# One level of Strassen for the second FFN product of two batches, and a new order of pieces, in an attention and FFN kernel

## The chip, the cores and the metric

The kernel runs on one core of a Trainium2 chip. The core has a matrix engine (PE; the loading of its stationary operand is listed as PEld), a vector engine (DVE), a scalar engine (ACT), a general engine (POOL) and a queue engine for transfers (SP). Each works through its own list of instructions in order and waits on semaphores for the others. SBUF is the on-chip memory, PSUM the eight banks into which PE writes. The metric is the device time of one execution in microseconds; of the kernel before there are three runs, with a median of 164.83 us (164.77 to 165.41).

## The reference

Eight batches of eight heads, 576 tokens, head dimension 64, 32 memory slots. With a softmax over the tokens, phi compresses keys and values to 32 rows; the queries attend to these; the outcome, 4608 tokens by 512, goes through a feed-forward network whose hidden layer is the maximum of three products.

```
a = exp(phi - max(phi, axis=2)); a = a / (sum(a, axis=2) + 1e-09)
k_m = einsum('bhsm,bhsd->bhmd', a, k);  v_m = einsum('bhsm,bhsd->bhmd', a, v)
scores = q @ k_m.T / sqrt(64);  attn = softmax(scores) @ v_m
x = attn.transpose(0, 2, 1, 3).reshape(4608, 512)
h = maximum(maximum(x @ w1, x @ w2), x @ w3)      # 512 -> 768
out = h @ w_out                                   # 768 -> 512, float32
```

## The kernel before

A batch is 576 tokens. Its compressed values are folded into the weights, so that the FFN works on the attention weights themselves: `fold` makes wp (for w1 - w3 and w2 - w3) and wp3 (for w3 times w_out), `ffn1` makes the hidden layer as max(a, max(b, 0)) of the differences, and `ffn2` adds the w3 part back: out = h @ w_out + attn @ wp3. In `ffn2` one tile of 128 tokens is eight matmuls of 512 columns in one PSUM bank: six over the hidden layer and two over attn. Each loads its own 128 by 128 stationary block. Two batches make 1152 tokens, nine tiles: T0 to T3 of each, and T4, which lies across both. A finished bank is copied to a tile `ot` in SBUF and stored by SP, 256 KB a tile.

The program is a written-out list of pieces, each a letter, a number and a batch: `F8@2` is step 8 of ffn1 for batch 2. Every engine executes its share of the pieces in the order of the list; nothing reorders them later. The pieces that matter here:

- L0, L1, L2, L3 load phi, K, V and q of a batch (L88 to L112). POOL issues them, so they stand in POOL's order with POOL's arithmetic. All loads go through one queue. H2, H0, Y and so on are the first batch's parts and the weights.
- E is the exponential of phi (ACT). r1 and r0 are POOL copies of V and K of batch 2 and later into an interleaved tile `kvr` (L102). B (PE) compresses K and V (for batches 0 and 1, in two parts straight from the loaded tile: B0 for K with the sums, B1 for V), N normalizes (DVE), K transposes on PE and copies.
- Q0 and Q1 transpose q (DVE), S are the scores (PE) and two exponentials (ACT); a, s, c are a transpose, a sum and a reciprocal (DVE) for each of two groups, m multiplies (POOL, L406), X transposes back into `attn` (DVE, L416).
- D0 to D3 are the folds, F0 to F11 ffn1 (an even one ends in a copy by ACT, an odd one in a maximum by DVE, both out of PSUM), T0 to T4 ffn2. O prepares w3 times w_out from the transposed w3 in `w3T`. U, A and P do not exist yet. A mark `!` swaps ACT for DVE or back in a piece that copies.
- A PSUM bank for each piece comes from a written-out string of digits.

A load may be issued only when what it overwrites has been read: K and V have two tiles, for even and odd batches, and phi and q two each. The loads of batch 2 overwrite what batch 0 used.

```
for w in """ ... """.split():
    n, b = w.rstrip("!").split("@")
    issue(int(b), n, w.endswith("!"))
```

## Time and profile before

| | us |
|---|---|
| median of three runs | 164.83 |
| span of the profiled execution | 163.3 |
| PE busy | 153.8 |
| ACT busy | 100.6 |
| DVE busy | 90.4 |
| POOL busy | 69.5 |
| ffn2's matmuls, 512 columns, L497 and L506 | 51.3 and 18.4 |
| ffn1's matmuls, L466 | 50.5 |
| V of batch 7 has landed | 111.8 |
| last matmul ends | 159.6 |

The page of the profiled execution gives its span, from the first to the last instruction, and no other time of it; the median of the runs lies 1.53 us above. All times inside the trace count from the span's start. A row of the timeline gives start, duration, engine, line, operation, output and inputs, and in brackets how long the engine stood idle before it and what ended that. A row of the stretches gives, behind the stretch's length, the busy time and the number of instructions of PE, PEld, DVE, ACT and POOL, then the granted clock of PE, the share of the DMA engines (above 1 where transfers overlap in one engine) and GB/s. A row of the chain gives start, duration and the work. Where a time of a named piece is given, it was found by counting PE's matmuls along the list. Landing times are the completion events of the transfers in the trace.

### The profile page before, as it was taken

The page shows a single profiled execution, that of the slowest core. Times are in us where ns is not written, and L with a number is a line of the kernel's source. Part 1 is how long each engine was busy: PE and PEld are TensorE (multiplying, and loading weights), DVE is VectorE, ACT ScalarE, POOL GpSimd, SP SyncE. Part 2 cuts the span into 40 slices and gives each one's busy share as a digit, 9 for nine tenths or more (in the row PEclk, how much of TensorE's full clock was granted, in tenths as well). Part 3 has the DMA queues.
Part 4 walks back from the last instruction along what each step waited for, and adds up shares of the span by engine and source line. Part 5 has one row for each costly group of instructions (what it writes and reads, how often), then busy time and mean ns, then how long its engine had stood idle before and what let it go on. Part 6 is the DMA issues. An engine that isn't in the chain of part 4 may idle for free.

```text
span 163.3 us, 4838 instructions
## 1 busy us (share of the span) xinstructions
PE 153.8 (94%) x2080; PEld 85.3 (52%) x2080; DVE 90.4 (55%) x181; ACT 100.6 (62%) x151; POOL 69.5 (43%) x71
## 2 busy tenths in 40 slices
PE   7978798899899999999999999999999999999990
PEld 2433444564377436743673575576553468744450
DVE  2023704798838665849399748879749128810010
ACT  4205445845497488778885899994658976223320
POOL 7932205100599259657968957646403100000000
PEclk9999999999999999999999999999999999999998
DMA  6999999999999999999999999996313130014333
GB/s 150 152 206 207 205 210 217 274 208 210 253 313 238 209 253 379 274 210 293 252 263 206 232 355 264 191 233 150 130 69 129 69 128 0 0 68 186 135 128 130
DMA packets 21974, 31.77 MB, mean 195 GB/s; under 512 B 1216, under 2 KB 16576, under 8 KB 21952
## 3 DMA queue, kind: packets, MB, share of 16 engines
q0 software_dynamic: 16080, 21.43, 68.7%
q1 hardware_dynamic: 5728, 9.90, 17.2%
q8 instruction: 16, 0.26, 0.6%
q10 hardware_dynamic: 144, 0.13, 0.2%
q14 instruction: 6, 0.05, 0.1%
HBM read 39.32 MB, written 9.44 MB: 299 GB/s over the span
## 4 chain that ended last, share of the span: by engine, by line
PE 83%; DMA 9%; POOL 2%; ACT 2%; issue 1%; DVE 1%; ACTq 0%; POOLq 0%
PE psum L497 29%; PE psum L466 28%; DMA wo_sb<-in_moe_w_out_dram 9%; PE psum L506 8%; PE psum L440 6%; PE psum L249 4%; PE psum L192 3%; PE psum L333 2%; PE psum L515 1%; ACT h L170 1%; PE psum L538 1%; PE psum L298 1%; POOL kvo L97 1%; ACT wp L172 1%; POOL qq L110 0%
## 5 line engine op out<-in xcount | busy, mean ns | idle before, releaser
L497 PE MATMUL psum<-wo_sb,hT 128*128 128x512 bf16 x210 | 51.3, 380 | 0.0
L466 PE MATMUL psum<-attn,wp 128*128 128x288 bf16 x384 | 50.5, 286 | 0.1
L479 DVE TENSOR_TENSOR hT<-psum,h 128x576 bf16<-128x576 f32 x48 | 34.2, 749 | 18.0 <-PE psum L466 12.5
L466 PEld LDWEIGHTS <-wp 128*128 128x128 bf16 x384 | 36.7, 98 | 13.2 <-issue 2.0
L172 ACT COPY ot<-psum 128x512 f32<-128x512 f32 x35 | 20.7, 591 | 32.1 <-PE psum L506 25.2
L497 PEld LDWEIGHTS <-hT 128*128 128x128 bf16 x210 | 19.2, 97 | 24.0 <-issue 4.3
L172 ACT CAST wp<-psum 128x1024 bf16<-128x1024 f32 (+1 forms) x31 | 29.2, 995 | 3.8 <-PE psum L440 2.0
L103 POOL COPY kvr<-kvo 128x2304 bf16<-128x2304 bf16 x12 | 25.3, 2111 | 13.7 <-DMA kvo<-in_k_dram 10.1
L170 ACT ACTIVATE h<-psum 128x576 bf16<-128x576 f32 x47 | 28.4, 659 | 3.5 <-PE psum L466 3.3
L409 POOL TENSOR_TENSOR t<-t,sm 128x576 bf16<-128x576 bf16 x14 | 16.1, 1154 | 24.6 <-DVE sm L404 24.4
L506 PE MATMUL psum<-wp,attn 128*128 128x512 bf16 x62 | 18.4, 379 | 0.0
L159 PE MATMUL psum<-warm 128*128 128x512 bf16 x44 | 12.1, 427 | 1.2 <-DVE warm L128 1.2
L313 DVE STREAM_TRANSPOSE qT<-qq 128x576 f32<-128x576 f32 x16 | 11.7, 747 | 1.4 <-DMA qq<-in_q_dram 1.4
L342 ACT ACTIVATE e<-psum 128x576 bf16<-128x576 f32 x16 | 9.6, 652 | 3.8 <-PE psum L333 3.8
L229 ACT ACTIVATE e<-ph 128x1152 bf16<-128x1152 f32 (+1 forms) x9 | 9.6, 1065 | 1.7 <-DMA ph<-in_phi_dram 1.6
L395 DVE TENSOR_REDUCE sm<-t 128x18 f32<-128x576 bf16 x14 | 10.3, 738 | 0.2
L387 DVE STREAM_TRANSPOSE t<-e 128x288 f32<-128x288 f32 x14 | 6.4, 465 | 6.2 <-ACT e L342 6.1
L97 POOL DMA_DIRECT2D kvo<-in_v_dram x9 | 6.7, 749 | 7.1 <-PE psum L249 4.1
L506 PEld LDWEIGHTS <-attn 128*128 128x128 bf16 x62 | 6.1, 98 | 7.1
L110 POOL DMA_DIRECT2D qq<-in_q_dram x8 | 6.2, 770 | 6.6 <-DVE h L174 3.7
L555 DVE COPY ot<-psum 128x256 f32<-128x256 f32 x1 | 0.4, 425 | 15.4 <-PE psum L546 15.4
L249 PEld LDWEIGHTS <-e 64*32 64x32 bf16 x720 | 6.9, 90 | 3.7 <-issue 3.3
(57 smaller groups left out, 114.4 us busy)
## 6 DMA issues: line engine op xcount, KB each, us to landing
out_dram<-ot SPq DMA_DIRECT2D x35, 256.0 KB, 5.6
qq<-in_q_dram POOLq DMA_DIRECT2D x8, 576.0 KB, 12.2
ph<-in_phi_dram POOLq DMA_DIRECT2D x7, 576.0 KB, 14.4
kvo<-in_k_dram POOLq DMA_DIRECT2D x7, 576.0 KB, 14.6
kvo<-in_v_dram POOLq DMA_DIRECT2D x7, 576.0 KB, 15.6
w_sb<-in_moe_w_dram POOLq DMA_DIRECT2D x3, 768.0 KB, 19.0
wo_sb<-in_moe_w_out_dram POOLq DMA_DIRECT2D x1, 768.0 KB, 14.6
ph<-in_phi_dram SPq DMA_DIRECT2D x2, 288.0 KB, 3.0
```

The costliest lines, as they stand in the source:

```text
L103: nc.gpsimd.tensor_copy(out=kvrs[b % 2][:, :, :, D * i : D * (i + 1)], in_=kvos[b % 2][:, 1 - i])
L159: nc.tensor.matmul(po[:, 0:BANK], lhsT=warm[:, 0:P], rhs=warm, start=True, stop=True)
L170: nc.scalar.activation(out=out_, in_=in_, func=AF.Relu)
L172: nc.scalar.copy(out=out_, in_=in_)
L249: nc.tensor.matmul(kvp[M * j : M * (j + 1), a, 0:nd], lhsT=s["e"][r, j, c, :], rhs={None: lambda: kvr[r, j, c, 0:nd], 0: lambda: k_and_one ...
L313: nc.vector.transpose(out=s["qT"][:, j].rearrange("p j c r e -> p (j c r e)").bitcast(FP32), in_=loaded[b]["q"][:, j].rearrange("p j c d - ...
L395: nc.vector.tensor_reduce(out=sm, in_=s["t", g].rearrange("p n r e -> p n e r"), op=ALU.add, axis=mybir.AxisListType.X,)
L409: nc.gpsimd.tensor_tensor(out=t, in0=t, in1=s["sm", g].unsqueeze(2).to_broadcast([P, S // HP, R, 2]), op=ALU.mult,)
L466: nc.tensor.matmul(acc[:, h, 0:SH], lhsT=wps[b][:, g, w * DF + ft * P : w * DF + (ft + 1) * P], rhs=attn[:, g, c0 : c0 + SH], start=(g == ...
L479: nc.vector.tensor_tensor(out=hT[:, ft, (b % 2) * S : (b % 2 + 1) * S].rearrange("p (h n) -> p h n", h=2), in0=a, in1=s["h1", ft], op=ALU.max,
L497: nc.tensor.matmul(po, lhsT=hT[:, fc, c0 : c0 + P], rhs=wo_sb[:, fc, :], start=(n == 0), stop=False,)
L506: nc.tensor.matmul(po, lhsT=attn[:, g, c0 : c0 + P], rhs=wp3s[b][:, g, :], start=False, stop=(g == NG - 1),)
```

## The change

For batches 5 and 6, T0 to T3 are replaced by seven products P0 to P6. The left matrix is the batch's four token tiles, 512 tokens by 1024 (768 of h and 256 of attn), the right one is w_out over wp3, 1024 by 512. Both are cut in two by two blocks: tokens into tiles 0 and 2 against 1 and 3, the inner dimension into 512 and 512 (three hidden tiles and one of attn each), the columns into 256 and 256. One level of Strassen's method in its form with fifteen additions needs seven block products for these in place of eight. A product is eight matmuls of 256 columns (four inner tiles by two token tiles).

What is new beside the products: U makes four differences of the blocks of w_out once (U0 to U3 at "batch 9", 768 elements in each partition, in the place of `w3T`, which is free after O0@0) and four of wp3 for each of the two batches (256 elements). A makes four sums or differences of h (A0 to A3, 768 elements) and four of attn (A4 to A7, 256 elements) for each batch. They are bf16; each runs on DVE or POOL as the list says: U on DVE where marked, A on POOL where marked. Three of the products' results are copied to SBUF while their bank goes on accumulating, three output blocks are made by a DVE addition of PSUM and such a copy, one by a plain copy. The store is two transfers of 512 KB a batch instead of four of 256 KB.

The tile of ones beside K and V moves ahead of K, and K and V change places in their tile; `opool` has four tiles in place of six. The order of pieces is a new one from N0@1 on, and the string of banks with it. The list's first pieces, up to N0@1, are unchanged. Shown are the new code, and of the two lists the old one's beginning of batch 1 and the new one from the same place on.

```diff
-    opool = ctx.enter_context(tc.tile_pool(name="opool", bufs=6))
+    opool = ctx.enter_context(tc.tile_pool(name="opool", bufs=4))
...
-    kvos = []
-    for i in range(2):
-        kvo = const.tile([P, 3, NP, NC, D], BF16, name=f"kvo{i}")
-        kvos.append(kvo)
+    KV = NP * NC * D
+    ones_k = [const.tile([P, D + 2 * KV], BF16, name=f"kvo{i}") for i in range(2)]
+    kvos = [
+        x[:, D:].rearrange("p (i j c d) -> p i j c d", i=2, j=NP, c=NC) for x in ones_k
+    ]
...
-            out=kv[:, 1 - i, h].rearrange("p j c d -> p j (c d)"),
+            out=kv[:, i, h].rearrange("p j c d -> p j (c d)"),
...
-            out=kvrs[b % 2][:, :, :, D * i : D * (i + 1)], in_=kvos[b % 2][:, 1 - i]
+            out=kvrs[b % 2][:, :, :, D * i : D * (i + 1)], in_=kvos[b % 2][:, i]
...
-    for kvo in kvos:
-        nc.vector.memset(kvo[:, 2, 0, 0], 1.0)
+    for x in ones_k:
+        nc.vector.memset(x[:, 0:D], 1.0)
...
-    def k_and_ones(kv, r, j, c):
-
-        flat = kv[r].rearrange("p i j c d -> p (i j c d)")
-        k0 = (NP * NC + j * NC + c) * D
-        step = 2 * NP * NC * D - k0
-        return flat[:, k0 : k0 + 2 * step].rearrange("p (i x) -> p i x", i=2)[:, :, 0:D]
+    def ones_and_k(b, r, j, c):
+        step = D + (j * NC + c) * D
+        return ones_k[b % 2][r, 0 : 2 * step].rearrange("p (i x) -> p i x", i=2)[:, :, 0:D]
...
+    KT = FT // 2
+    CH = DM // 2
+    TW = 2 * P
+    SUB, ADD = ALU.subtract, ALU.add
+    B11, B12, B21, B22 = [
+        (slice(KT * i, KT * (i + 1)), slice(CH * j, CH * (j + 1)))
+        for i in range(2)
+        for j in range(2)
+    ]
+    tw = w3T.rearrange("p f j n -> p (f j n)").rearrange("p (i k c) -> p i k c", i=4, k=KT)
+    sa0 = const.tile([P, 4, TW], BF16, name="sa0")
+    oj0 = [const.tile([P, 2, DM], FP32, name=f"oj{i}") for i in range(2)]
+    SNAP = {0: "m5", 1: "m1", 4: "u2"}
+    twb, sas, quads = {}, {}, {}
+    def combine(on_dve, out_, in0, in1, op):
+        eng = nc.vector if on_dve else nc.gpsimd
+        eng.tensor_tensor(out=out_, in0=in0, in1=in1, op=op)
+    def combine_w(b, i, on_dve):
+        if b == B + 1:
+            x = {n: wo_sb[:, n[0], n[1]] for n in (B11, B12, B21, B22)}
+            t = [tw[:, n] for n in range(4)]
+        else:
+            if b not in twb:
+                twb[b] = work.tile([P, 4, CH], BF16, name="twb")
+            w = wp3s[b]
+            x = {n: w[:, n[0].start // KT, n[1]] for n in (B11, B12, B21, B22)}
+            t = [twb[b][:, n] for n in range(4)]
+        in0, in1 = [(x[B12], x[B11]), (x[B22], t[0]), (x[B22], x[B12]), (x[B21], t[1])][i]
+        combine(on_dve, t[i], in0, in1, SUB)
+    def sums(b):
+        if b not in sas:
+            if b == B - 1:
+                s = inp.tile([P, NP, NC, D], BF16, name="sx", tag="qq")
+                s = s.rearrange("p j c d -> p (j c d)").rearrange("p (i n) -> p i n", i=3)
+                sa = inp.tile([P, NP, NC, D], BF16, name="sy", tag="qq")
+                sa = sa.rearrange("p j c d -> p (j c d)")[:, 0 : 4 * TW]
+                sa = sa.rearrange("p (i n) -> p i n", i=4)
+            else:
+                s, sa = w_sb[:, 0:3, 2], sa0
+            sas[b] = (
+                s.rearrange("p i (k q n) -> p i k q n", k=KT, q=2),
+                sa.rearrange("p i (q n) -> p i q n", q=2),
+            )
+        return sas[b]
+    def blocks(x, b, k):
+        c0 = (b % 2) * (S + HP)
+        x = x[:, :, c0 : c0 + 2 * TW]
+        return [
+            [
+                x[:, k * i : k * (i + 1)].rearrange("p f (q r n) -> p f q r n", q=2, r=2)[
+                    :, :, :, r
+                ]
+                for i in range(2)
+            ]
+            for r in range(2)
+        ]
+    def combine_a(b, i, on_dve):
+        s, sa = sums(b)
+        n = i % 4
+        if i < 4:
+            (a11, a12), (a21, a22) = blocks(hts[b // 2], b, KT)
+            t = {0: s[:, 0], 1: s[:, 1], 2: a21, 3: s[:, 2]}
+        else:
+            (a11, a12), (a21, a22) = blocks(attns[b // 2], b, 1)
+            t = {m: sa[:, m : m + 1] for m in range(4)}
+        in0, in1 = [(a21, a22), (t[0], a11), (a11, a21), (a12, t[1])][n]
+        combine(on_dve, t[n], in0, in1, ADD if n == 0 else SUB)
+    def products(b, i, swap):
+        s, sa = sums(b)
+        h, a = blocks(hts[b // 2], b, KT), blocks(attns[b // 2], b, 1)
+        wp3 = wp3s[b]
+        def plain(r, c):
+            return lambda k, q: h[r][c][:, k, q] if k < KT else a[r][c][:, 0, q]
+        def summed(n):
+            src = h[1][0] if n == 2 else s[:, min(n, 2)]
+            return lambda k, q: src[:, k, q] if k < KT else sa[:, n, q]
+        def w_plain(i, j):
+            c = slice(CH * j, CH * (j + 1))
+            return lambda k: wo_sb[:, KT * i + k, c] if k < KT else wp3[:, i, c]
+        def w_summed(n):
+            return lambda k: tw[:, n, k] if k < KT else twb[b][:, n]
+        lhs, rhs, name = [
+            (summed(0), w_summed(0), "y"),
+            (plain(0, 0), w_plain(0, 0), "x"),
+            (plain(0, 1), w_plain(1, 0), "z"),
+            (summed(3), w_plain(1, 1), "y"),
+            (summed(1), w_summed(1), "x"),
+            (summed(2), w_summed(2), "x"),
+            (plain(1, 1), w_summed(3), "x"),
+        ][i]
+        acc = quads.setdefault(b, {})
+        if i < 3:
+            acc[name] = one_bank()
+        po = acc[name]
+        for k in range(KT + 1):
+            for q in range(2):
+                nc.tensor.matmul(
+                    po[:, q * CH : (q + 1) * CH],
+                    lhsT=lhs(k, q),
+                    rhs=rhs(k),
+                    start=(i < 3 and k == 0 and q == 0),
+                    stop=(k == KT and q == 1),
+                    skip_group_check=True,
+                )
+        x = po.rearrange("p (q n) -> p q n", q=2)
+        def copy(out_, in_):
+            if swap:
+                nc.vector.tensor_copy(out=out_, in_=in_)
+            else:
+                nc.scalar.copy(out=out_, in_=in_)
+        if i in SNAP:
+            t = ln if i == 0 else work.tile([P, S], FP32, name="snap", tag="r")
+            t = acc[SNAP[i]] = t[:, 0:DM].rearrange("p (q n) -> p q n", q=2)
+            copy(t, x)
+        if i == 2:
+            if b == B - 1:
+                ot = [inp.tile([P, NP, NC, M], FP32, name=f"ox{n}", tag="ph") for n in range(2)]
+                acc["ot"] = [
+                    x.rearrange("p j c m -> p (j c m)")[:, 0 : 2 * DM].rearrange(
+                        "p (q n) -> p q n", q=2
+                    )
+                    for x in ot
+                ]
+            else:
+                acc["ot"] = oj0
+        if i not in (2, 4, 5, 6):
+            return
+        ot = acc["ot"][i // 5][:, :, slice(0, CH) if i in (2, 6) else slice(CH, DM)]
+        if i == 6:
+            copy(ot, x)
+        else:
+            if i == 4:
+                x = acc["y"].rearrange("p (q n) -> p q n", q=2)
+            y = acc[{2: "m1", 4: "u2", 5: "m5"}[i]]
+            nc.vector.tensor_tensor(out=ot, in0=x, in1=y, op=ADD)
+        if i in (4, 6):
+            r0 = b * S + (b % 2) * HP
+            rows = out[r0 : r0 + 2 * TW].rearrange("(q r p) c -> p q r c", q=2, r=2)
+            nc.sync.dma_start(out=rows[:, :, i // 5], in_=acc["ot"][i // 5])
 
...
+            "U": lambda: combine_w(b, i, swap),
+            "A": lambda: combine_a(b, i, not swap),
+            "P": lambda: products(b, i, swap),
...
-        L0@1 V1@0 F1@0 E@1 F3@0 L1@1 F5@0 F9@0 F7@0 L3@1 F11@0 B0@1 T3@0 N0@1 K0@1! L2@1 Q1@1
-        L2@2 L1@2 Q0@1 L0@2 V2@0 T0@0! L3@2 S@1 T1@0 a0@1 s0@1 c0@1 m0@1 B1@1 N1@1 a1@1 L1@3
-        K1@1 s1@1 D0@1 D1@1! D2@1 c1@1 m1@1 X0@1 L3@3 r1@2 X1@1 T2@0! L2@3 F6@1 F10@1 F7@1 F2@1
-        F3@1 F4@1 F0@1 r0@2 E@2 F5@1 F1@1 F11@1 L0@3 L0@4 F8@1 L2@4 F9@1 B@2 D3@1 N@2 Q1@2
-        T0@1! K@2 T2@1! r0@3 Q0@2 S@2 a0@2 a1@2 s1@2 c1@2 m1@2 T4@1! D1@2! s0@2 D2@2 c0@2 m0@2
-        X1@2 D0@2 T3@1 Q0@3 L3@4 X0@2 Q1@3 T1@1 F0@2 F4@2 F8@2 F6@2 F9@2 E@3 F7@2 r1@3 F5@2
...
+        D2@0 D4@0 F4@0 L0@1 V1@0 F1@0 E@1 F3@0 L1@1 F5@0 F9@0 F7@0 L3@1 F11@0 B0@1 T3@0
+        N0@1 U0@9 Q0@1 Q1@1 K0@1 V2@0 T0@0 S@1 L2@1 B1@1 a0@1 T1@0 s0@1 L0@2 N1@1 c0@1
+        a1@1 K1@1 s1@1 c1@1 m1@1! D0@1 L2@2 L1@2 m0@1 L3@2 D1@1! X0@1 X1@1 D2@1! T2@0!
+        F6@1 F4@1! F10@1 F0@1! F7@1 E@2 r1@2 F8@1 L1@3 F11@1 F5@1 F1@1 F9@1 F2@1 r0@2
+        F3@1 B@2 D3@1 T0@1! N@2 K@2! Q1@2 L2@3 Q0@2 T2@1 L0@3 S@2 a0@2 a1@2 s0@2 T4@1!
+        L0@4 D1@2! s1@2 D2@2! E@3 c0@2 D0@2 T1@1 L3@3 T3@1 L2@4 r0@3 r1@3 D3@2 B@3 c1@2
+        m1@2! X1@2 m0@2 X0@2 F8@2 F2@2 N@3 Q0@3 F3@2 F4@2 F6@2 Q1@3 F5@2 F0@2 F9@2 F1@2
+        F10@2 F7@2 F11@2 K@3 E@4 T2@2 L3@4 Q1@4 S@3 a0@3 T1@2 L1@4 L2@5 a1@3 s1@3 c1@3
+        L3@5 L0@5 D1@3! r1@4 D0@3 L1@5 L0@6 Q0@4 r0@4 D2@3 s0@3 m1@3 c0@3 L1@6 T0@2!
+        m0@3! D3@3 B@4 X1@3 L2@6 T3@2 X0@3 F8@3 U2@9 N@4 F4@3 L3@6 K@4! Q0@5 F5@3 F9@3
+        F10@3 r1@5 F0@3 F11@3 S@4 F1@3 F2@3 a1@4 r0@5 a0@4 F6@3 U1@9 F3@3 E@5 F7@3 s0@4
+        D0@4 D1@4! c0@4 T3@3 B@5 s1@4 c1@4 m0@4 D3@4 D2@4 m1@4 r0@6 X0@4 T0@3! X1@4 F4@4
+        N@5 F10@4 Q1@5 L0@7 L1@7 F5@4 F0@4! r1@6 F8@4 F11@4 F2@4 K@5 U3@9 F6@4 E@6 F9@4
+        L2@7 S@5 T4@3! Q1@6 Q0@6 D2@5 a1@5 a0@5 s0@5 D3@5 B@6 L3@7 T2@3! N@6 s1@5 F3@4
+        r0@7 c0@5 c1@5 F7@4 m1@5 F1@4 K@6! E@7 T1@3! S@6 a0@6 U0@5! m0@5 D1@5! T0@4!
+        X1@5 s0@6 D0@5! X0@5 D1@6! D3@6 r1@7 T3@4 F4@5 a1@6 B@7 Q0@7 D2@6 s1@6 D0@6 U0@6
+        N@7 A4@5! T1@4 c1@6 m1@6 F5@5 F8@5 F2@5 F6@5! F9@5 U1@5 A5@5 K@7! F0@5 F7@5 F1@5
+        F3@5 F10@5 F11@5 T2@4! Q1@7 A7@5! A0@5 X1@6 D0@7! U2@6! S@7 c0@6 a1@7 s1@7 T4@5!
+        U2@5 D2@7 D3@7 A6@5! A1@5! A2@5 a0@7 m0@6 A3@5! D1@7! U3@5 P0@5! P1@5! X0@6
+        P2@5! P3@5 F2@6 s0@7 c1@7 c0@7 m1@7! m0@7 A4@6! P4@5 F4@6 X1@7 F6@6 P5@5 A5@6!
+        X0@7 F10@6 A6@6 F3@6 F8@6 P6@5 F9@6 F5@6 F0@6 F11@6 F10@7 F7@6 F1@6 F2@7 A7@6!
+        F8@7! A0@6! F4@7 F11@7 U1@6 F9@7 F3@7 F5@7 P0@6! F0@7! F6@7! A1@6! A3@6 F1@7
+        P1@6 P2@6! A2@6 F7@7 P3@6! P4@6 T0@7! T4@7! T1@7! P5@6! T2@7! U3@6 P6@6! T3@7
```

## The prediction

> **What bounds the kernel now.** I read the page's busy shares first, then busy times by stretch, then GpSimd (POOL) in order of time, then the chain.
>
> ```profile
> span 163.3 us, 4838 instructions
> PE 153.8 (94%) x2080; PEld 85.3 (52%) x2080; DVE 90.4 (55%) x181; ACT 100.6 (62%) x151; POOL 69.5 (43%) x71
> DMA  6999999999999999999999999996313130014333
> ```
>
> PE is busy 94%, but the DMA row is full too, up to slice 27 (about 112 us). So there are two near-bounds. The stretches:
>
> ```profile
> 38.00:42.00 4.00, 4.00 (x86) 1.64 (x83) 3.45 (x5) 2.41 (x6) 0.00 (x0) 1.00 1.21 210
> 46.00:159.60 113.60, 113.56 (x1451) 65.03 (x1449) 68.04 (x135) 78.76 (x117) 52.44 (x43) 1.00 0.78 191
> 116.40:159.60 43.20, 43.18 (x405) 23.69 (x383) 16.31 (x29) 23.58 (x37) 2.27 (x2) 1.00 0.26 95
> 159.60:163.30 3.70, 0.00 (x0) 0.00 (x0) 0.00 (x0) 0.37 (x1) 0.00 (x0) 0.78 0.32 109
> ```
>
> From 46 us to the end PE idles 0.04 us of 113.6: whatever it must wait for lengthens the kernel, whatever it need not compute shortens it. The DMA share of 1.21 at 38 to 42 us is a full load queue. POOL feeds that queue and also multiplies:
>
> ```profile
> 24.74 0.74 POOL L97 DMA_DIRECT2D kvo<-in_v_dram  x1 [4.08 <-PE psum L249]
> 25.47 0.75 POOL L97 DMA_DIRECT2D kvo<-in_k_dram  x1
> 26.79 0.75 POOL L93 DMA_DIRECT2D ph<-in_phi_dram  x1 [0.57 <-issue]
> 31.21 0.74 POOL L110 DMA_DIRECT2D qq<-in_q_dram  x1 [3.66 <-DVE h L174]
> 42.42 1.16 POOL L409 TENSOR_TENSOR t<-t,sm 128x576 bf16<-128x576 bf16 x1 [10.47 <-DVE sm L404]
> 43.53 0.80 POOL L97 DMA_DIRECT2D kvo<-in_k_dram  x1
> 44.45 1.15 POOL L409 TENSOR_TENSOR t<-t,sm 128x576 bf16<-128x576 bf16 x1
> 46.35 2.12 POOL L103 COPY kvr<-kvo 128x2304 bf16<-128x2304 bf16 x1
> 49.14 2.12 POOL L103 COPY kvr<-kvo 128x2304 bf16<-128x2304 bf16 x1
> ```
>
> All four loads of batch 2 (V, K, phi, q) are issued by 32 us; then POOL stands 10.47 us in front of m0@1. Under that wait the queue works: by the trace's completion events q1 lands at 37.69, V1 40.53, V2 44.11, K2 48.47, phi2 50.03, q2 53.47, and so on without a gap to V7 at 111.80 and q7 at 114.64. The packs r1@2 and r0@2 (46.35, 49.14) end at 51.26; B@2 starts at 51.94, when the twelve F@1 are done. Matmul prices, from the chain:
>
> ```profile
> 146.82 0.43 PE psum L506 x2
> 152.43 1.29 PE psum L497 x6
> 157.73 0.76 PE psum L538 x6
> 158.49 0.22 PE psum L546 x2
> ```
>
> A 512-column matmul takes 0.215 us, a 256-column one 0.11 (the 0.76 has a 0.1 us start in it), although each loads its own weights.
>
> **The change, part by part.** *Products.* Per batch 4 tiles x 8 x 0.215 = 6.91 us go and 7 x 8 x 0.11 = 6.14 us come: minus 0.77, for two batches minus 1.53 us, all on PE. L538 has the same size and weight pattern, so I take 0.11. The new order also changes less often between 128-row and tiled pieces (0.1 us each): minus 0.2.
>
> *Combinations.* A 768-element difference costs 0.56 us on DVE (from 1024 elements in 0.684 and 2048 in 1.198), 1.54 on POOL (from 576 in 1.154); 256 elements 0.3 and 0.5. From about 110 us on POOL gains 12 us of these (12 x 0.5, 4 x 1.54), DVE 3.4, 4 us of PSUM additions (6 x 0.67, from 0.749 for 576) and 2.5 of copies. The third stretch above has 41 us of POOL and 27 of DVE free; cost 0. If a product waited for its last difference, it would be A1 then A3 (POOL, 3 us after A0, 1.15 more for m0@6): up to 1.5 us per batch. That is the upper bound; the lower is 0. PSUM reuse between products has 0.9 to 2.6 us of other matmuls against a copy of 0.59. The four differences of w_out (U@9, 1.54 each on POOL) lie among the loads: U0@9 and U1@9 are followed below, U2@9 and U3@9 stand in front of L3@6 and L2@7, which the full queue hides; without it 1.5 us each.
>
> *Small parts.* The ones beside K instead of behind V: B@0 and B@1 keep 72 matmuls of 128 columns, 0. Four output tiles in place of six: a T comes each 1.73 us at most, four in 6.9, a store lands in 5.6 (median) or 7.6 (the longest): 0, at worst 0.7 for a copy. T0@0, T2@1 and T2@2 are copied by DVE (0.67) and not by ACT (0.59): no PSUM bank of theirs is wanted within 0.9 us, 0.
>
> *Order before B@2: what decides.* The new POOL order is L3@1, U0@9, L2@1, L0@2, **m1@1**, L2@2, L1@2, **m0@1**, L3@2, r1@2, L1@3, r0@2. U0@9 waits for O0@0 (26.3 on PE) and takes 1.54, so L2@1 is issued at 28 instead of 19.92; as K1 and q1 still hold the queue until 37.69, V1 lands at 40.5 as before, phi2 at 42.1. But V2 and K2 now stand behind m1@1. That needs q1 (37.69), two transposes, S@1, the exponentials and, in DVE's new order, a0, s0, N, c0, a1, the K1 copy, s1, c1. T1@0 now runs between B1@1 and K1@1 on PE, so the K1 copy is at 43.4, c1 ends at 44.65. m1@1 runs 44.75 to 45.9, L2@2 is issued at 45.9, L1@2 at 46.65, m0@1 ends at 48.55.
> Two consequences. X0@1 needs m0@1: F6@1 starts at 49.1, not 45.96; PE stands still for 2.9 us. And the load queue is empty from 42.1. From issue to first packet the first load took 2.44 us (1.25 to 3.69), and a full load behind another runs 2.84 (37.69 to 40.53 for V1): V2 lands at 51.2, r1@2 ends at 53.4; L1@3 0.75; K2 landed at 54.0; r0@2 ends at 56.3. The F@1 end at 55.1. **B@2 starts at 56.4, plus 4.5 us.** Bounds: F6@1 alone gives 55.1 (plus 3.2); 1 us more in the queue gives 57.4.
> The Trainium skill ("DMA: Bandwidth & Descriptors", section on the anatomy of one DMA) gives about 2.0 us plus bytes over 436 GB/s for a GpSimd-issued DMA. As an estimate that puts V2's 1.18 MB at 50.6 and the sum 0.6 us lower; the trace's first load, above, speaks for the longer figure.
>
> *Order after B@2.* Old work left on PE is 159.58 - 51.94 = 107.64 us; new 107.64 - 1.53 - 0.2 = 105.9. So PE ends at 162.3 without further waits. Further waits by the same bookkeeping: E@3 on ACT now stands before D0@2's copy and waits for phi3 (66), so T3@1's copy and F8@2 slip 0.5; q3 is issued behind phi3 and phi4 and lands near 71.5, and DVE's Q0@3 is in front of F3@2's maximum: 0.4; m0@3 stands behind r0@4 (K4, 81), m1@3 and L1@6: F8@3 slips 0.7; m0@4 and m1@4 behind U1@9: F4@4 slips 0.4. Sum 2.0. A second way: the load queue of the old trace has no gap to make up time in, so the 3.5 us by which q2 is late (57.0 against 53.47) reach V7: it lands at 115.3, r1@7 ends at 117.4 and B@7 starts then. The new list has 46.8 us of PE pieces from B@7 on (35 F 17.2, 14 products 12.3, 8 T 14.5, the rest 2.8): 164.2, that is 1.9 us of further waits. I take 1.9, as the stream is the harder limit. Bounds 0 (the stretch above shows no PE wait of this kind) and 4.
>
> *The end* stays: T3@7 in two halves, 3.7 us from PE's last matmul to the span's end. P6@6's 512 KB go out on SP 1.4 us before; the old T4@7 put 256 KB there. 0 to 0.5; I take 0, since the last half leaves from ACT's queue.
>
> Sum: plus 4.5 - 1.7 + 1.9 = plus 4.7 us; the span goes from 163.3 to 168.0. The median of the runs is 164.83, 1.53 above the span of the profiled execution; with that distance kept, **169.5**.
>
> **Rivals.**
> *The saving arrives (faster).* If V2 and K2 are packed by the old 51.26, only minus 1.7 us remain: 163.1. It needs POOL free of m1@1 before about 40 us. For it: the queue runs ahead everywhere else. Against it: m0@1 in the old order, with less in front of it, could not start before 42.42. Chance 0.07. A halved wait (plus 2.2 at B@2, nothing after) gives 165.3, no change: 0.04.
> *The load stream falls further back.* Between B@2 and B@7 the old trace has 64.5 us, the new pieces at their prices 58.9 (37 F of 0.49, 14 T of 1.73, 2 T4 of 1.94, the small pieces and changes 12.7): the new order wants V7 sooner after B@2 than the old. With 3.5 us of lag V7 is just what B@7 waits for; each further us that POOL's packs lose it, standing before later loads until their own data land, is a us at the end. With 3 us more: 172.5. Chance 0.1.
> *Products wait for differences late.* 1.5 us per batch on top of the forecast: 172.5. For: DVE holds F maxima beside them. Against: the free time above. Chance 0.07.
> *PE's clock falls in the 2.9 us gap.* In the last stretch the mean granted clock is 0.78 of 3.70 us, which is 2.1 us at 1.00 and then 0.50: it fell 2.1 us after the last matmul. In the gap at F6@1 3.4 us at half clock would stretch the F@1 to 56.8; B@2 then slips only 0.4, since it waits for r0@2 anyway: 169.9. It is counted inside the forecast, at evens.
> The Trainium skill ("TensorE: Matmul & The Clock Gate", Part 1) has the clock halve after an idle window of about 3.4 us; by that rule a 2.9 us gap would leave it whole and the time at 169.5. The 2.1 us of the trace speak against waiting that long.
>
> **How the numbers follow.** The forecast with its bounds has 0.72: 169.5, own range 166.3 (B@2 at plus 3.2, no later wait) to 172.6 (plus 5.5, later waits 4). The stream (0.1) and the late products (0.07) end at 172.5; 0.04 is no change, 0.07 faster. The range 166.2 to 172.6 leaves out the last two and the upper halves of the two before, 2 in 10. Within 0.5% (0.8 us) is about what a measurement here cannot tell from no change. Faster 0.07, same 0.04, slower 0.89.
>
> **What will show it.** POOL's L2@2 after the first multiplication of batch 1 and near 46 us; a gap of PE of about 3 us before the first F@1 and of 1 us before B@2, ended by a copy on POOL; B@2 near 56.4; product matmuls of 256 columns 0.11 us apart; PE's end near 164. Wrong if L2@2 is issued before 42 us, if B@2 starts before 54, or if the products run at more than 0.12 us a matmul.

## The result, and the profile after

The changed kernel takes 174.64 us (median of four runs, 174.00 to 175.26), the kernel before beside it 164.91 (164.77 to 165.41): 1.056 times as long, interval 1.049 to 1.063. The forecast was 169.5 with 166.2 to 172.6 about it: the sign is right, the size is not, and the time lies above the range. The profiled execution is the longest of the four, 0.6 us above their median. Of the runs below, one with two issues moved (172.07 us) and one with both batches' products (172.64 us) were over 1.5% slower than the fastest of their kernel; the medians take in all runs, the ratios leave these two out.

The page of the changed kernel, its span, busy times, granted clock and DMA row:

```profile
span 173.3 us, 4949 instructions
PE 156.0 (90%) x2128; PEld 91.2 (53%) x2128; DVE 109.2 (63%) x211; ACT 92.0 (53%) x135; POOL 90.5 (52%) x91
PEclk9999999999978999999999999999999999999999
DMA  5999999996199999999999999999310303200635
```

The DMA row, solid before up to slice 27, now has a hole, above all at slice 10 counted from 0 (43 to 48 us): the load queue ran empty. Just behind it the clock dips. POOL in order of time shows why the queue was empty:

```profile
26.70 1.64 POOL L503 TENSOR_TENSOR w3T<-wo_sb 128x768 bf16<-128x768 bf16 x1 [8.77 <-PE psum L193]
28.30 0.78 POOL L98 DMA_DIRECT2D kvo<-in_v_dram  x1
...
45.05 1.15 POOL L409 TENSOR_TENSOR t<-t,sm 128x576 bf16<-128x576 bf16 x1 [15.22 <-DVE sm L404]
46.16 0.79 POOL L98 DMA_DIRECT2D kvo<-in_v_dram  x1
46.94 0.75 POOL L98 DMA_DIRECT2D kvo<-in_k_dram  x1
...
52.85 2.10 POOL L104 COPY kvr<-kvo 128x2304 bf16<-128x2304 bf16 x1 [3.25 <-DMA kvo<-in_v_dram]
...
56.26 2.11 POOL L104 COPY kvr<-kvo 128x2304 bf16<-128x2304 bf16 x1 [0.62 <-DMA kvo<-in_k_dram]
```

POOL stands 15.22 us in front of m1@1, and only then issues V and K of batch 2. V2 lands at 52.80, K2 at 56.20. What PE waits for, the rows of its timeline with idle time in front:

```profile
49.52 7.87 PE L466 MATMUL psum<-attn,wp 128*128 128x288 bf16 x48 [2.79 <-DVE attn L417]
58.42 0.80 PE L248 MATMUL psum<-kvr,e 64*32 64x129 bf16 x72 [1.02 <-POOL kvr L104]
...
85.80 0.80 PE L248 MATMUL psum<-kvr,e 64*32 64x129 bf16 x72 [0.73 <-POOL kvr L104]
89.38 1.42 PE L466 MATMUL psum<-attn,wp 128*128 128x288 bf16 x8 [0.94 <-DVE rden L268]
93.75 0.65 PE L466 MATMUL psum<-attn,wp 128*128 128x288 bf16 x4 [0.82 <-DVE hT L479]
```

These are F6@1, B@2, B@4, F8@3 and F11@3. Before, PE stood still for 0.04 us in all from 46 us to its end. By stretches (columns as before), first the gap and what follows, then B@2 to B@7 and B@7 to PE's end:

```profile
46.80:49.50 2.70, 0.00 (x0) 0.01 (x1) 0.60 (x2) 0.56 (x1) 2.69 (x4) 1.00 0.66 64
49.50:53.00 3.50, 3.48 (x16) 2.29 (x17) 2.11 (x3) 1.22 (x3) 0.25 (x2) 0.55 1.14 223
58.42:122.47 64.05, 60.34 (x971) 32.63 (x970) 45.27 (x93) 45.73 (x65) 49.35 (x41) 1.00 1.13 246
122.47:169.54 47.07, 46.97 (x484) 32.80 (x483) 34.42 (x61) 21.12 (x33) 18.66 (x20) 1.00 0.22 81
```

Where the time went, by the start of pieces on PE:

| | before | after | step |
|---|---|---|---|
| B0@1 starts | 35.04 | 35.97 | +0.93 |
| B0@1 to B@2 | 16.91 | 22.45 | +5.54 |
| B@2 to PE's end | 107.63 | 111.12 | +3.49 |
| PE's end | 159.58 | 169.54 | +9.96 |

The first row is no part of the change: the pieces up to there are the old ones, w3 (the piece Y2) landed at 16.90 in place of 15.83 in this execution, PE waited for it, and kernels below with the same beginning start B0@1 between 34.7 and 36.4.

### The profile page after: what moved, and what is told of

Its sections match the earlier page's. It is cut to its first block, busy times and chain, and to the rows that moved or that the text cites. A ratio compares the mean times of both kernels' runs of the same rounds, so it can differ in the third digit from the quotient of the medians.

```text
span 173.3 us, 4949 instructions
## 1 busy us (share of the span) xinstructions
PE 156.0 (90%) x2128; PEld 91.2 (53%) x2128; DVE 109.2 (63%) x211; ACT 92.0 (53%) x135; POOL 90.5 (52%) x91
## 4 chain that ended last, share of the span: by engine, by line
PE 39%; DMA 36%; POOL 13%; issue 9%; DVE 1%; ACT 1%; POOLq 0%; ACTq 0%
DMA kvo<-in_v_dram 17%; PE psum L466 13%; PE psum L655 10%; DMA kvo<-in_k_dram 10%; DMA wo_sb<-in_moe_w_out_dram 9%; PE psum L598 7%; POOL kvr L104 4%; PE psum L664 2%; POOL kvo L98 2%; POOL t L409 2%; PE psum L440 2%; POOL qq L111 1%; PE psum L248 1%; POOL w3T L503 1%; PE psum L673 1%
## 5 line engine op out<-in xcount | busy, mean ns | idle before, releaser
L466 PE MATMUL psum<-attn,wp 128*128 128x288 bf16 x384 | 53.0, 292 | 5.9 <-DVE attn L417 3.0
L655 PE MATMUL psum<-wo_sb,hT 128*128 128x512 bf16 x162 | 39.8, 380 | 0.1
L171 ACT ACTIVATE h<-psum 128x576 bf16<-128x576 f32 x40 | 25.0, 652 | 18.8 <-PE psum L466 17.9
L655 PEld LDWEIGHTS <-hT 128*128 128x128 bf16 x162 | 14.2, 98 | 18.8 <-issue 4.6
L173 ACT COPY ot<-psum 128x512 f32<-128x512 f32 x22 | 13.0, 590 | 18.9 <-PE psum L664 13.3
L417 DVE STREAM_TRANSPOSE attn<-t 128x288 f32<-128x288 f32 x14 | 6.5, 471 | 11.5 <-POOL t L409 11.5
L664 PE MATMUL psum<-wp,attn 128*128 128x512 bf16 x46 | 13.7, 379 | 0.0
L440 PE MATMUL psum<-w_sb,kvt 64*32 64x512 bf16 (+1 forms) x200 | 8.2, 373 | 0.6 <-DVE kvt L177 0.3
L98 POOL DMA_DIRECT2D kvo<-in_k_dram x9 | 6.9, 764 | 2.9 <-DMA qq<-in_q_dram 2.1
L160 PEld LDWEIGHTS <-warm 128*128 128x128 bf16 x44 | 4.5, 109 | 7.1 <-issue 3.0
```

The costliest lines, as they stand in the source:

```text
L160: nc.tensor.matmul(po[:, 0:BANK], lhsT=warm[:, 0:P], rhs=warm, start=True, stop=True)
L171: nc.scalar.activation(out=out_, in_=in_, func=AF.Relu)
L173: nc.scalar.copy(out=out_, in_=in_)
L440: nc.tensor.matmul(ps[M * j : M * (j + 1), a, 0 : hi - lo], lhsT=lhs[r, M * j : M * (j + 1)], rhs=rhs[r, j, :], start=(i == 0), stop=(i == ...
L466: nc.tensor.matmul(acc[:, h, 0:SH], lhsT=wps[b][:, g, w * DF + ft * P : w * DF + (ft + 1) * P], rhs=attn[:, g, c0 : c0 + SH], start=(g == ...
L655: nc.tensor.matmul(po, lhsT=hT[:, fc, c0 : c0 + P], rhs=wo_sb[:, fc, :], start=(n == 0), stop=False,)
```

## The experiments

The theory from the prediction: V2 and K2, issued behind m1@1, cost what B@2 slips; the rest is waits of the new order, and the products do their small part. Each kernel below undoes or does one part. Times are medians, with the ratio to the kernel before on the same chip.

**Loads early, in the new order.** The changed kernel with five issues moved:

```diff
- N0@1 U0@9 Q0@1 Q1@1 K0@1 V2@0 T0@0 S@1 L2@1 B1@1 a0@1 T1@0 s0@1 L0@2 N1@1 c0@1
- a1@1 K1@1 s1@1 c1@1 m1@1! D0@1 L2@2 L1@2 m0@1 L3@2 D1@1!
+ N0@1 L2@1 L2@2 L1@2 L0@2 L3@2 U0@9 Q0@1 Q1@1 K0@1 V2@0 T0@0 S@1 B1@1 a0@1 T1@0 s0@1 N1@1 c0@1
+ a1@1 K1@1 s1@1 c1@1 m1@1! D0@1 m0@1 D1@1!
```

> The changed kernel with five load issues moved: V1, V2, K2, phi2 and q2 are issued by POOL ahead of the difference U0@9 and of the multiplications m1@1 and m0@1; everything else, the products too, stays. Theory (the late issue of batch 2's loads is the cause): V2 lands near 44 and K2 near 48, PE's gap before F6@1 shrinks from 2.9 us to about 1.3 (m0@1 still comes after m1@1), the clock stays whole, B@2 starts near 54 instead of 58.4; 168 to 170 us in all. Rival (the new order starves on its loads later whatever happens at batch 2, because it wants V7 5.6 us sooner): B@2 comes early but the gain is given back before B@7, 172 or more. Rival (products and differences cost the time): nothing changes, 174 to 175.

Measured: 169.45 us, ratio 1.026 (1.022 to 1.030). POOL, and the one wait of PE before B@2:

```profile
44.89 2.27 POOL L409 TENSOR_TENSOR t<-t,sm 128x576 bf16<-128x576 bf16 x2 [11.67 <-DVE sm L404]
47.10 2.11 POOL L104 COPY kvr<-kvo 128x2304 bf16<-128x2304 bf16 x1
49.95 2.12 POOL L104 COPY kvr<-kvo 128x2304 bf16<-128x2304 bf16 x1
```

```profile
47.82 6.25 PE L466 MATMUL psum<-attn,wp 128*128 128x288 bf16 x48 [1.26 <-DVE attn L417]
```

V2 lands at 43.02, the packs follow the multiplications at once, B@2 starts at 54.01, 18.2 us behind B0@1 in place of 22.45, the clock stays whole. But 63.07 us lie between B@2 and B@7, where the pieces at their prices need 58.9: 4.2 us of waits remain there without any late load of batch 2. They are not quite the same ones: B@4, F11@3 and the maximum behind q3 wait no more, F8@3 (0.95) and F4@4 (0.69) do, and F4@5 (0.89) is new.

**Only V and K of batch 2.** `c1@1 L2@2 L1@2 m1@1! D0@1 m0@1 L3@2`: the two issues pass one multiplication.

> The changed kernel with two load issues moved over one multiplication: V2 and K2 are issued right before m1@1 instead of right behind it; V1, U0@9, phi2 and q2 stay where the change put them. Theory (that m1@1 stands in front of these two issues is the whole of the early loss): both are issued near 30 us, V2 lands near 45, K2 near 49; m0@1 follows m1@1 directly, F6@1 starts near 47.8, B@2 near 54, and the time is that of the first experiment, 169.5 (168.5 to 170.5). Rival (V1 behind U0@9, or q2's late issue, has a part): 171 to 174.

Measured: 170.13 us, ratio 1.027 (1.022 to 1.033), as with all five moved. F6@1 waits 1.25 us and B@2 starts 18.6 us behind B0@1. Two issues of 0.75 us, moved ahead of one multiplication of 1.15 us that waits 15 us for its input, are worth nearly half of the change's loss.

**Late loads in the old order.** The kernel before, with V, K and q of batch 2 issued behind m1@1 (here the second of the two multiplications, in the change the first), phi of batch 2 ahead of them, and K and q of batch 3 set back so that they stay behind them:

```diff
- K0@1! L2@1 Q1@1 L2@2 L1@2 Q0@1 L0@2 V2@0 T0@0! L3@2 S@1 ... c1@1 m1@1 X0@1 L3@3 r1@2 ... L0@4
+ K0@1! L2@1 L0@2 Q1@1 Q0@1 V2@0 T0@0! S@1 ... c1@1 m1@1 L2@2 L1@2 L3@2 X0@1 r1@2 L1@3 ... L0@4 L3@3
```

> The kernel before with only POOL's loads of batch 2 moved: V2, K2 and q2 are issued behind m1@1, phi2 right behind V1, K3 behind r1@2 and q3 behind phi4. No product, no difference, no other piece moved. Theory (late issue of these loads): V2 lands near 52.5, K2 near 56, r0@2 ends near 58, B@2 starts near 58 instead of 51.9; no gap before F6@1, since m0@1 and m1@1 come first; 171 us (169.5 to 173). Rival (the products or the order elsewhere are the cause): within 2 us of the kernel before, 165 to 167.

Measured: 175.97 us, ratio 1.066 (1.063 to 1.069): the loads alone cost more than the whole change, and about twice what was expected. F6@1 starts at 45.42 without a gap; PE then ends the twelve F@1 and stands:

```profile
57.22 1.18 PE L249 MATMUL psum<-kvr,e 64*32 64x129 bf16 x72 [5.76 <-POOL kvr L103]
```

V2, issued at 45.00, landed at 51.21 (6.2 us), K2 at 55.01; the pack ended at 57.17. The clock was granted at half from 53.81 for 6.83 us. B@2 comes 22.7 us behind B0@1 (16.91 before), B@7 68.95 us behind B@2 (64.51). Of these 4.4 us, 2.76 are a second wait, at F0@2: DVE's Q0@3 waits for q of batch 3, issued at 58.60 and landed at 71.71 (59.09 before), and X0@2, which F0@2 needs, stands behind Q0@3. So the early loss is shown by the 5.8 us at B@2; part of the rest belongs to the load of batch 3 that this experiment itself set back.

**The clock in the gap.** The changed kernel with twelve useless matmuls in front of F6@1 (`T2@0! Z12@0 F6@1`), which write a bank that nobody reads.

> The changed kernel with twelve matmuls of no use (512 columns on a zero tile, 2.6 us) in PE's gap in front of F6@1; nothing else differs. Theory A (the half clock after the gap costs nothing, since B@2 waits for the pack of K2 anyway): the granted clock stays at 1.00 through the twelve F@1, they end 1.7 us earlier, B@2 still starts near 58.4, and the time is 174 to 175.5. Theory B (the half clock is a loss of its own): 172.5 to 173.

Measured: 174.62 us, ratio 1.056 (1.051 to 1.062): nothing gained. By stretches:

```profile
46.00:49.50 3.50, 3.29 (x17) 1.45 (x16) 0.94 (x3) 0.70 (x2) 3.25 (x4) 1.00 0.66 71
49.50:53.00 3.50, 3.50 (x31) 2.77 (x30) 2.89 (x4) 2.72 (x4) 0.71 (x1) 1.00 1.15 228
53.00:57.30 4.30, 2.40 (x19) 1.65 (x17) 3.56 (x6) 0.82 (x2) 3.68 (x3) 1.00 1.22 209
```

With the gap filled the clock stays at 1.00 (0.55 in the changed kernel, from 49.50 to 53.00), the F@1 end at 55.4, and B@2 still waits for the pack: 57.87. The gap and the half clock lie beside the wait for K2.

**The new order without products.** The changed kernel with T0 to T3 of batches 5 and 6 in the places of P0, P2, P4 and P6, without U, A and the rest of P.

> The changed kernel without its products and differences: batches 5 and 6 get T0 to T3 with 512 columns again, placed where P0, P2, P4 and P6 stood and in their banks; all else keeps the new order. Theory (the order costs, the products save 1.5 us and their differences nothing): U0@9 no longer stands in front of V1, but m1@1 still stands in front of V2, so B@2 stays near 58; 175.5 to 176.5 us, 1 to 2 us slower than the changed kernel. Rival (the products and differences cost): 165 to 170.

Measured: 177.02 us, ratio 1.073 (1.069 to 1.077). The order costs the change its 12 us; the products then give 2.4 back. Its stretch from B@7 to PE's end:

```profile
120.53:171.47 50.94, 48.80 (x430) 28.06 (x435) 25.01 (x44) 23.26 (x37) 4.58 (x4) 1.00 0.23 84
```

PE is busy 48.80 us there against 46.97 with products, so the products alone are worth 1.8, the 1.7 of the prediction; the other 2.1 us of this stretch are idle time of PE, mostly waits for ACT to copy a finished bank (0.72 twice and 0.29), in a tail that was not made for these tiles. Between B@2 and B@7 this kernel needs 62.95 us, the changed one 64.05 (63.69 with the gap filled): without the four differences of w_out on POOL it issues V7 at 106.12 in place of 110.23, that is 3.3 us sooner counted from B@2.

**Products in the old order, one batch.** The old list, with the differences and sums of batch 6 behind m0@7 and the last F, and its products among the last tiles:

```diff
+ ... X1@7 m0@7 U0@9 U1@9 U2@9 U3@9 D1@7! T1@4 ... F5@6 U0@6 U1@6 U2@6 U3@6 A4@6! A5@6! A6@6! A7@6! F10@6 ...
+ F9@6 F1@6 F3@7 A0@6 A1@6 A3@6 T3@5 A2@6 P1@6 P2@6 P0@6 T0@7! P3@6 T2@7! P4@6 T1@7 P5@6 T4@7! P6@6! T3@7
```

> The order of the kernel before, with its banks, and the seven products for batch 6 alone, put among the last pieces, the differences on POOL and DVE where these are idle (POOL behind m0@7, DVE behind the last F). Theory (products of 256 columns run at 0.11 us a matmul and their additions and copies are hidden): minus 0.77 us, 164.1 (163.7 to 164.6). Rival (the products wait for their copies or differences): 165 to 167.

Measured: 164.13 us (163.69 to 164.92), ratio 0.994 (0.992 to 0.996): 0.6% faster than the kernel before, a small gain but clear of the interval, and faster than the changed kernel.

```profile
PE 151.5 (93%) x2084; PEld 87.7 (54%) x2104; DVE 95.1 (59%) x189; ACT 99.9 (61%) x150; POOL 81.1 (50%) x83
```

From B@7 (116.55) to PE's end (158.89) it is 42.34 us in place of 43.13, 0.79 less: the price of 0.77 for a batch, seven products of 0.87 us in place of four tiles of 1.73.

**Products in the old order, both batches.** The same for batches 5 and 6, behind T0@4, in two arrangements: the second has DVE's differences of batch 5 behind X0@7 and five of its products in the tail. The first:

```diff
+ ... Q0@7 B@7 m1@6 U0@9 U0@5 A4@5! N@7 X1@6 P1@5 P2@5 K@7 A0@5 A5@5! A7@5! T3@4 Q1@7 A1@5 S@7 A3@5 U1@9 U1@5 a0@7 ...
+ ... c0@7 F4@6 T4@5! D3@6 D2@7 D0@7! P0@5 T1@4 A2@5 m0@7 U2@5 A6@5! D3@7 D2@6 X1@7 D1@7! P3@5 P4@5 X0@7 F6@7 ...
```

> The order of the kernel before up to T0@4, unchanged, and the products of both batches behind that: P1 and P2 of batch 5 in the place of T2@5, P0 where T0@5 stood, the rest of batch 5 among the following F, batch 6 in the tail as in the experiment with batch 6 alone; all differences behind the last pack. Theory (the order cost everything and the products save what their columns say): 163.3 (162.8 to 163.9), 0.8 us less than with batch 6 alone. Rival (the products need the room that the new order makes, their differences and additions hold PE up): 164.5 to 167.

> Once more both batches' products in the order of the kernel before, with what the second-to-last experiment taught: of batch 5 only P1 and P2 (no differences) stand where T2@5 stood, T1@4 and F8@6 fill the place of T0@5, all differences that DVE makes come behind X0@7, and P0 and P3 to P6 of batch 5 go to the tail among T0, T2, T1, T4 of batch 7. In the run with 170.3 us, DVE's differences stood in front of the softmax of batch 7. Theory (products cost what their columns say if their differences stand in front of nothing urgent): 163.4 (162.9 to 164.2). Rival (there is no room on DVE and in PSUM for two batches in the old order): 165 or more.

Measured: 170.30 us, ratio 1.029 (1.024 to 1.034), and 170.90, ratio 1.033 (1.030 to 1.037). Both missed by 7 us. In the first, PE's rows behind B@7 with the longest waits:

```profile
123.63 0.65 PE L466 MATMUL psum<-attn,wp 128*128 128x288 bf16 x4 [1.24 <-ACT h L171]
134.68 1.15 PE L466 MATMUL psum<-attn,wp 128*128 128x288 bf16 x8 [2.09 <-DVE attn L417]
149.76 0.83 PE L598 MATMUL psum<-wo_sb,hT 128*128 128x256 bf16 x6 [0.71 <-DVE hT L479]
```

The products hold banks over many pieces, the folds and F get fewer and wait for ACT's copies; DVE's differences stand ahead of the softmax of batch 7, so X0@7 is late; and they take longer than alone (1.30, 0.91 and 0.78 us for what takes 0.55 alone). The second arrangement shows the same three kinds of wait (1.11 and 0.82 us for ACT, 1.30 for X0@7, 1.28 for a maximum); from B@7 to PE's end it takes 48.70 us, where 41.6 (42.34 less another 0.77) would be its price. So the old order has room for one batch's products, not in these two ways for two. Other arrangements were not tried: that two batches need a new order is made likely, not shown.

**The later waits: differences among the loads.** The loads-early kernel with U0 to U3 of w_out behind r1@7.

> The kernel of the first experiment (batch 2's loads early), and the four differences of w_out (U0 to U3 at batch 9, 1.64 us each on POOL) moved from among the loads to behind the last pack r1@7. Theory (after batch 2 the order loses because each batch's multiplications stand behind packs and these differences on POOL): the waits in front of F4@4 (0.9 us) and F8@3 get shorter, 168.5 (167.5 to 169); the waits behind packs stay. Rival (the differences among the loads cost nothing, as the prediction had it): 169.5 as without the move.

Measured: 168.76 us, ratio 1.023 (1.016 to 1.029), 0.4% below the loads-early kernel and inside its interval. B@2 to B@7 is 62.87 us against 63.07: where the loads are early, the four differences cost next to nothing in all. The theory's step is seen at F4@4, whose wait is gone; but F8@3 still waits 0.95 us, and B@4 (0.34) and F11@3 (0.36) wait too in this execution.

**The later waits: a multiplication behind a load.** The loads-early kernel with m0@3 ahead of L1@6 (`m1@3 c0@3 T0@2! m0@3! L1@6`).

> The kernel with the early loads, with one step moved on POOL: m0@3 stands ahead of L1@6 (K of batch 6) and no longer behind it. With the early loads alone m1@3 ran from 79.62, L1@6 from 80.73, m0@3 from 81.56, X0@3 started at 82.76 and F8@3 waited 0.95 us. Theory (the prediction's step on F8@3: m0@3 stands behind r0@4, m1@3 and L1@6): m0@3 starts at 80.8, X0@3 at 82.0, F8@3's wait falls to 0.2, and the time by 0.7 to about 168.7; K of batch 6 is issued 1.2 us later and nothing waits for it. Rival: the 0.7 us come back as a wait at F10@4 or F4@5, which wait for DVE, and the time stays at 169.2 to 169.5.

Measured: 170.05 us, ratio 1.031 (1.027 to 1.034): no gain. The wait at F8@3 is gone, and there are two others:

```profile
80.94 0.80 PE L248 MATMUL psum<-kvr,e 64*32 64x129 bf16 x72 [0.68 <-POOL kvr L104]
88.11 0.65 PE L466 MATMUL psum<-attn,wp 128*128 128x288 bf16 x4 [0.87 <-DVE hT L479]
```

B@4 waits for the pack of K4, F11@3 for a maximum behind Q0@5, which DVE begins when q5 has landed (86.61). The wait at B@4 is not of the move's making: the pack of K4 and its load stand ahead of m0@3 on POOL, and K4 landed 1.2 us later in this execution (78.72 against 77.50), B@2 0.5 later. The wait at F11@3 is one that F8@3's had covered: with two issues moved, q5 landed as late behind B@2 (32.5 us, here 32.1), F8@3 waited, and F11@3 did not. So the rival holds in substance, at another place than it named. The profiled execution has B@2 to B@7 in 62.50 us, 0.57 less than with the loads early, but that is not the move's doing: F4@5's wait is missing too, for the reason told in the next experiment.

**The later waits: a difference beside a pack.** In the loads-early kernel DVE's 256-element difference U0@5 took 1.87 us and X0@5 came late. It was moved behind X0@5 (`D0@5! X0@5 U0@5! D1@6!`).

> The kernel with the early loads, with one step moved: U0@5, DVE's difference of 256 elements, stands behind X0@5 and no longer ahead of X1@5. With the early loads alone it took 1.87 us (112.01 to 113.88), while POOL copied V of batch 7 into kvr (r1@7, 111.63 to 113.74); in the changed kernel, where it began 0.2 us before that copy, 0.45; beside no POOL work 0.25 to 0.28. Theory: such a difference and a POOL copy cannot run beside each other, the one that comes second waits for the first to end, and the 1.6 us are the cause of the 0.89 us by which F4@5 waits for X0@5. Then U0@5 now takes under 0.5 us, X0@5 starts near 114.2 in place of 115.96, F4@5's wait is gone, B@7 comes 0.9 us sooner behind B@2 (62.2 us in place of 63.07), and the time falls from 169.4 to about 168.5. Rival 1: the 1.87 us are the difference's own (a wait for its wp part counted as duration): it stays that long behind X0@5, F4@5's wait is gone all the same. Rival 2: X0@5 is late for another reason (the exponentials of batch 6 in front of s0@6): F4@5's wait stays at 0.5 or more and the time at 169.4.

Measured: 169.12 us, ratio 1.026 (1.023 to 1.029), the same as with the loads early. In the profile F4@5's wait is gone and B@2 to B@7 is 62.30 us, 0.77 shorter, as the theory says; but the medians do not show it. And the run tells less than it was to: V7 landed 2 us later here (113.72), the pack began at 113.77, so U0@5 would have been clear of it in its old place too, as it was in the kernel with m0@3 moved, where it took 0.25 us unmoved. What stands is the pair of lines, loads-early first (POOL, then DVE), then this kernel:

```profile
111.63 2.11 POOL L104 COPY kvr<-kvo 128x2304 bf16<-128x2304 bf16 x1 [0.64 <-DMA kvo<-in_v_dram]
```

```profile
112.01 1.87 DVE L503 TENSOR_TENSOR twb<-wp 128x256 bf16<-128x256 bf16 x1
```

```profile
115.82 0.25 DVE L503 TENSOR_TENSOR twb<-wp 128x256 bf16<-128x256 bf16 x1
```

Begun inside the pack, the difference ended 0.14 us after it. It took 1.92 us in the kernel with the differences late, and 0.25 in the changed kernel (not the 0.45 of the expectation, which is another difference's) and in three others, where it began ahead of the pack. Rival 1, that the length is its own, falls.

## Why the prediction was right and wrong

*Right: the place and the mechanism of the loss.* m1@1 at 45.05 (forecast 44.75), V2 issued at 46.16 (45.9), F6@1 at 49.52 (49.1) behind a gap of 2.79 us (2.9), B@2 1.02 us behind the F@1 (1), ended by a copy on POOL. That two issues behind one multiplication carry it is shown in the new order: moved back they give 4.5 of the 9.7 us. The old order confirms it for the group: V, K and q of batch 2 issued late set B@2 back by 5.8 us.

*The clock: undecided, and without weight.* Whether it would fall was given evens, at 0.4 us. It fell, and with the gap filled the time was the same.

*Right: products, combinations at the end, small parts.* 0.87 us for a product (8 x 0.11); 47.07 us from B@7 to PE's end against 46.8; 3.8 us from there to the span's end against 3.7. POOL's differences took 1.64 and 0.67 us each where 1.54 and 0.5 were reckoned, and PE did not wait for them. The rival of late products did not come.

*Wrong in size: "V2 lands at 51.2".* The step put together 2.44 us to the first packet and 2.84 for the transfer, 5.3 in all. V2 took 6.64 with nothing ahead of it in the queue and K2 another 3.40 (forecast 2.8); in the old order with late loads 6.2 and 3.8. The bound of "1 us more in the queue" was thus the value. That is plus 1.04 us at B@2 (5.54 in place of 4.5). The trace tells which part was mis-sized. V2's first packet moves at 47.66, 1.50 us behind the issue, so the start was shorter than the 2.44 taken. The transfer was longer, 5.14 us in place of 2.84. The stretches to the first packet, the microsecond behind it, and the rest up to the landing (GB/s over all queues is the last figure):

```profile
46.16:47.66 1.50, 0.57 (x3) 0.08 (x1) 0.00 (x0) 0.89 (x2) 1.50 (x3) 1.00 0.04 11
47.66:48.66 1.00, 0.00 (x0) 0.00 (x0) 0.00 (x0) 0.00 (x0) 0.99 (x2) 1.00 0.89 50
48.66:52.80 4.14, 3.27 (x15) 2.14 (x16) 2.71 (x4) 1.02 (x2) 0.94 (x2) 0.64 1.11 200
```

The queue that had run empty moved 50 GB/s at first, where the full one of before moved 210 (38.00 to 42.00). After that V2 shared the rate with 0.19 MB of stores and with 0.10 MB of K2 (up to V2's landing the load queue moved 0.69 MB, V2 is 0.59). The forecast took the full queue's rate for the empty one. With the loads late in the old order it was much the same: 1.5 us to the first packet, 4.7 of transfer. Why the transfer begins so slowly is not shown.

As an estimate by the Trainium skill ("DMA: Bandwidth & Descriptors", the anatomy of one DMA), V2 would have landed at 50.6 from the issue as forecast, or at 50.9 from the issue as measured, still further from the 52.80 than the forecast.

*Wrong, and the largest: "I take 1.9, as the stream is the harder limit", with 4 as the upper bound.* The waits between B@2 and B@7 come to 5.2 us (64.05 against 58.9). PE's rows show 3.7 of it as idle time; the rest is mostly the 0.16 us by which a piece otherwise starts before the one ahead of it has ended. Counted from start to start, over the same sequence in the kernel before, the four steps that were named came to 2.6 us against 2.0: F8@2 0.24 (forecast 0.5), the maximum behind q3 0.60 (0.4), F8@3 1.12 (0.7), F4@4 0.67 (0.4). F8@2 came by another way than the one named: its row is ended by DVE's X0@2, not by a copy on ACT. Missing from the forecast were B@4 (0.92, waits for the pack of K4, landed at 83.59, 6.3 us later than before), F11@3 (0.99, behind Q0@5, which waits for q5, landed at 92.25) and S@3 (0.27). The stream was followed to its last load alone, where it did not bind: V7's pack ended at 120.77, B@7 began at 122.47. It bound at K4 and q5, in the middle. And its lag was not the 3.5 us of q2 but 6.3 at K4 and 6.8 at V7 (118.61 against 111.80): a pack that waits for its load holds the next issues, which is the rival "the load stream falls further back", given 0.10. Its 172.5 was too low as well.

*Wrong: these waits put down to the late stream.* With the stream back in time (V7 at 111.58) there were still 4.2 us of waits in place of 5.2. So most of the loss behind B@2 does not need the late stream. The new order wants B@4 25.3 us behind B@2, where the old one has 29.8; with early loads it comes to 25.7, and even there B@4 starts (79.72) just as K4's pack ends (79.67), though K4 landed as early as before (77.50 against 77.30). The single waits have causes that were tested: F8@3's goes when m0@3 is moved, F4@4's when the differences among the loads are, and F4@5's, in one execution, was a difference on DVE held up by a pack on POOL. But none of these moves shortened the kernel beyond its interval. Which piece of the order is to blame for the whole is not settled.

*Wrong in one place: differences at cost 0.* Where the loads were late, the kernel without products issued V7 3.3 us sooner behind B@2 and ran B@2 to B@7 in 62.95 us against 63.69 and 64.05: 0.7 to 1.1 us, the "1.5 each" that was named for a queue with no cover, in part. With early loads they are nearly hidden (0.2).

*Not foreseen: 0.93 us* at the start of batch 1 in the profiled execution, behind weights that landed late; kernels with the same beginning do not all show it, so it is put down to the execution and not to the change. Not all of it need have reached B@2: with the gap filled B0@1 began 0.97 us sooner and B@2 only 0.55. As the starts of pieces divide it, with 1.04 at B@2 and 3.3 of later waits it makes the 5.3 us between the forecast's 168.0 of span and 173.3.

## What to carry to other kernels

Where an engine both computes and issues transfers in order, an issue moved behind an instruction that waits is delayed until that wait ends, and every later load with it: price the move by the time of that wait, then follow the stream to each load that the new order wants sooner, not only to the last. A saving of block products (0.8 us of PE for one batch) is real and can be had alone, by adding it to the order that runs well; a new order for its sake must first be shown to cost less than that. Waits of a tight order are not a sum that can be paid off one by one: removing the one at F8@3 uncovered one behind it, and other waits came and went between executions with landings that differ by 1 to 2.5 us (K4 77.5 to 78.7, V7 111.6 to 114.1).

## What the runs showed of the hardware that was not expected

*A clock that changes at fixed steps of 3.41 us.* PE idle for 2.79 us (changed kernel) and 2.09 (first arrangement of both batches) was followed by half clock for 3.41 us, and 5.76 us by 6.83, twice that. But after 2.45 us (gap filled, ahead of B@2) and 2.76 (loads late, ahead of F0@2) the clock stayed whole, as after 1.26. So the length of a gap alone does not decide. In the changed kernel the stretches between two changes last 44.37, 3.41 and 119.47 us, 13, 1 and 35 times 3.41, and the clock fell 0.3 us after work had begun again. Laid out in such steps, the last one before the fall holds 0.62 us of matmuls in the changed kernel. The two closest cases are these, the first with the loads late, where the clock stayed, the second with both batches' products, where it fell at the end of the step:

```profile
70.88:74.29 3.41, 1.37 (x12) 1.09 (x12) 1.80 (x3) 0.62 (x2) 1.80 (x2) 1.00 1.17 242
132.30:135.72 3.42, 1.33 (x12) 0.85 (x11) 1.08 (x2) 1.55 (x3) 2.54 (x4) 1.00 0.16 60
```

In these runs a step with 1.33 us of matmuls or less was followed by half clock, one with 1.37 or more by the whole. The same gap can thus cost the clock or not, by where it lies in the steps. The Trainium skill ("TensorE: Matmul & The Clock Gate", Part 1) has a window of 3.4 us that runs freely and halves the clock when idle; the length and the fixed steps agree with the traces, but that a whole window must be idle does not.

*DVE and POOL exclude each other in differences.* The 256-element difference on DVE took 1.87 us inside a POOL copy that had begun first, 0.25 where it began ahead of one; in the second arrangement of both batches a 768-element one took 1.84 us beside POOL's difference, where 0.55 is its time alone:

```profile
139.06 1.63 POOL L503 TENSOR_TENSOR w3T<-wo_sb,w3T 128x768 bf16<-128x768 bf16 x1
```

```profile
139.27 1.84 DVE L503 TENSOR_TENSOR hT<-hT 128x768 bf16<-128x768 bf16 x1
```

It ended at 141.11, 0.42 us after POOL's. DVE's reductions and its maxima out of PSUM keep their 0.74 and 0.76 us inside a POOL copy. The Trainium skill ("SBUF — State Buffer", Who interferes with whom) says that a DVE instruction with two SBUF inputs and a POOL instruction that reads SBUF share a port, and that the later one waits in full; the rows agree but for about 0.1 us, by which both ended sooner than a full wait and their own time would give. In the changed kernel's own execution no difference lost more than 0.2 us on DVE or 0.3 on POOL by it.
